# Another order for the start of a fused attention and two-MoE kernel: the first pair of heads, zero matmuls, planner keys

## The chip, the cores and the metric

The kernel runs on one core of a Trainium2 chip. The metric is the device time of one execution in microseconds (us), lower is better. Engines are named as in the profile: PE (TensorE, with PEld for its weight loads), DVE (VectorE), ACT (ScalarE), POOL (GpSimd) and SP (SyncE, which here issues nearly all DMAs).

## The reference, cut to what matters

```python
q_rot, k_rot = rotate(q), rotate(k)            # (4, 8, 576, 64): 4 batches, 8 heads
scores = (q_rot @ k_rot.T) / sqrt(64)
attn = softmax(scores)                          # over the keys
x = (attn @ v), heads put side by side          # (2304, 512)
x = relu(x @ w_in) ** 2 @ w_out                 # dense layer, 512 -> 2048 -> 512
e = argmax(x @ w_gate)                          # 8 experts, one for each token
y = gate * eom * (relu(x @ w1[e]) @ w2[e])      # 512 -> 1024 -> 512
```

`rotate` multiplies by cosines and sines of the position. All is float32; the kernel splits most operands into a high and a low part in a shorter format ("fp32r" in the rows) and multiplies high by high, high by low and low by high.

## The kernel before, in words

**Attention.** The 32 heads are taken as 16 pairs. `prepare(p)` (L272) makes a pair's operands, `unit(P, p, c)` (L405) works on one chunk of its queries (five chunks a pair, `QC`). For a pair, `prepare` loads k and q transposed, 128 partitions by 576 (`load`, L281: k is slot 2 of the tile `x`, q slot 0), makes a copy with neighbouring partitions exchanged (`swap`, DVE, L289), multiplies both with the table of cosines and the table of sines (`mul`, twice each, L292) and adds (`add`, L296). For all pairs but the first the multiplications and the addition run on POOL, for the first on DVE. Then k is split: `high_k` on ACT and `low_k` on POOL write the tile `hl`, and `fan` (L328), four DMAs of 288 KB a pair, copies both parts to the two halves of the partitions of the operand tile `d`. q is split straight into `d` (`high_q`, `low_q`). v is loaded, split in the same way (`v_high`, `v_low`), and two small copies `ends_` fill the tile `dz` for the last chunk. The first pair differs: its k goes without `fan`; four ACT casts (`first_high`, L320, 64 partitions each) and four DVE subtractions (`first_low`, L324) write all quarters of `d` directly. Both tables come in one DMA of 576 KB (L287), and one ACT instruction scales them for q (L335).

**A unit.** Four matmuls of 288 columns make the scores of one head (`scores`, L416, two PSUM buffers), DVE takes the least (`least`, L435), ACT the exponential (L439), PE transposes the result by the tile `ident` (L473, L479), ACT and DVE evacuate it as high and low part (L487, helper lines L209 and L212), and PE multiplies with v (L572).

**After the attention.** The dense layer runs over five blocks of tokens (`add_block`, L731). The first block's input is loaded and put together by POOL (L770 to L783) once all pairs are prepared, since it takes the place of the preparing tiles (`gate0`, L1415). Its weights come as raw words and are converted by ACT and DVE in the attention's shadow (`add_conversion`, L665). Then come routing and the experts.

**The order of the work** is made by a planner (`Plan`, L125). Every piece of work is added with its engine, an assumed cost, a key, what it depends on, and the buffers (rings) it uses. `emit` plays the pieces through: whichever engine is free first takes, among its pieces that are ready by then plus a small allowance, the one with the least key:

```python
t = max(free.get(e, 0.0), min(ready[n] for n in some))
n = min((ops[n][3], n) for n in open_[e] if ready[n] <= t + AHEAD.get(e, 0))[1]
```

The result is only an order of instructions for each engine. On the chip each engine runs its own list strictly in that order, and waits at an instruction whose data isn't there. The keys are `KEYS[class]` plus a small number that rises with the pair and the chunk, so a class with a lower value in `KEYS` goes ahead of another whenever both are ready. `fanned` (L344, L388, L657) is a dependency for the planner alone: loads of later pairs and of the constants follow the first pair's rotated k in the plan. The constants' split (`split`, L648, on DVE) is one piece with an assumed cost of 0.8 us.

Of the kernel before, what the change touches and what calls it, by code (L numbers as in the profile page):

```python
# [9 lines left out]
F32 = mybir.dt.float32  # L10
# [5 lines left out]
AF = mybir.ActivationFunctionType  # L16
# [5 lines left out]
B, H, S, D = 4, 8, 576, 64  # L22
# [33 lines left out]

def f32(ap):
    return ap.bitcast(F32)
# [6 lines left out]
def dve(n):  # L65
    return 67 + n / 0.96


def dves(n):
    return Shared(dve(n))  # L70
# [6 lines left out]
def act(n):  # L77
    return 93 + n / 1.2
# [6 lines left out]
def pool2(n):  # L85
    return 130 + 2.18 * n
# [18 lines left out]
def sub_price(on, n):  # L105
    return ("DVE", dves(n)) if on == "v" else ("POOL", pool2(n))
# [18 lines left out]
class Plan:  # L125
# [72 lines left out]
def two_moe_kernel(ctx, tc, qk, v, tab, cst, w_in, w_out, wg, w1, w2, out):  # L198
    nc = tc.nc
    te, ve, se, po, sp = nc.tensor, nc.vector, nc.scalar, nc.gpsimd, nc.sync  # L200
# [10 lines left out]
    def sub(eng, out, a, b):  # L211
        eng.tensor_tensor(out=out, in0=a, in1=b, op=ALU.subtract)  # L212
# [7 lines left out]
    pools, rings, plan = {}, {}, Plan()  # L220
# [8 lines left out]
    ident = rt.tile([128, 128], F32, name="ident")  # L229
# [20 lines left out]
    def add_attention(ctx, rest, first):  # L250
# [4 lines left out]
        ps_1 = pool(ctx, "ps_1", 1, space=PSUM)  # L255
# [3 lines left out]
        tabs = pre.tile([128, 4, S], F32, name="tabs")  # L259
# [9 lines left out]
        ring_z = plan.ring(1)  # L269
        zeros = [plan.add("DVE", 150, lambda: ve.memset(f32(ends_q), 0.0), -1000, [], [])]  # L270

        def prepare(p):  # L272


# [45 lines left out]
            def first_high(j, u):  # L320
                h, o = slice(64 * j, 64 * j + 64), slice(64 * u, 64 * u + 64)
                se.copy(out=operand()[o, j, 1], in_=T["x"][h, 2])

            def first_low(j, u):  # L324
                h, o = slice(64 * j, 64 * j + 64), slice(64 * u, 64 * u + 64)
                sub(ve, operand()[o, j, 2], T["x"][h, 2], f32(T["d"][h, j, 1]))
# [10 lines left out]
            on, split = ("vvvvvv", "aavvap") if first else (choice(ROPE, p, 6), choice(SPLIT, p, 6))  # L337
            eng = lambda i: ve if on[i] == "v" else po
            price = lambda i: ("DVE", dves(S)) if on[i] == "v" else ("POOL", pool2(S))
            hls, ds = ring_hl.take(), ring_d.take()  # L340
            parts = {}
            for i in (1, 0):
                k = key + KEYS["rope"] - i
                o = plan.add("SP", 3670 if first and i else 1220, lambda i=i: load(i), key + KEYS["load"] - i, fanned, [xs])  # L344
                if first and i:
                    tables = plan.add("ACT", act(2 * S), scale_tables, key + KEYS["qk"], [o], [])
                ready = [tables] if first and not i else []
                m = [plan.add("DVE", dve(S), lambda i=i: swap(i), key + KEYS["swap"] - i, [o], [xs])]
                m.append(plan.add(*price(3 * i), lambda z=2 * i: mul(z), k, [o, m[0], *ready], [xs]))
                m[0] = plan.add(*price(3 * i + 1), lambda z=2 * i + 1: mul(z), k, [m[0], *ready], [xs])  # L350
                o = plan.add(*price(3 * i + 2), lambda i=i: add(i), k, m, [xs])
                k = key + KEYS["qk"] - i
                if i and first:
                    T["fan"] = []
                    for j in range(2):
                        made_ = []
                        for u in range(2):
                            a = plan.add("ACT", act(S), lambda j=j, u=u: first_high(j, u), k, [o], [xs, ds])
                            made_ += [a, plan.add("DVE", dves(S), lambda j=j, u=u: first_low(j, u), k, [a], [xs, ds])]
                        T["fan"].append(made_)  # L360
                    fanned.append(o)
                elif i:
                    a = plan.add(*copy_price(split[1], S), high_k, k, [o], [xs, hls])
                    b = plan.add(*sub_price(split[3], S), low_k, k, [a], [xs, hls])
                    T["fan"] = [[plan.add("SP", 2444, lambda j=j: fan(j), key + KEYS["fan"], [a, b], [hls, ds])] for j in range(2)]
                else:
                    T["q"] = []
                    for j in range(2):
                        e = split[0] + split[2] if j == 0 else SECOND[2 * (p % (len(SECOND) // 2)):][:2]
                        if first:  # L370
                            e = "av" if j else "av"
                        a = plan.add(*copy_price(e[0], S), lambda j=j, e=e: high_q(j, e[0]), k, [o], [xs, ds])
                        b = plan.add(*sub_price(e[1], S), lambda j=j, e=e: low_q(j, e[1]), k, [a], [xs, ds])
# [14 lines left out]
            r = plan.add("SP", 1430, load_v, key + KEYS["load"], fanned, [vrs])  # L388
# [220 lines left out]
        made = {0: prepare(0), 1: prepare(1)}  # L609
        for p in range(NP):  # L610
            P = made.pop(p)
            for c in range(5):
# [956 lines left out]
```

## Time and profile before

| | us |
|---|---|
| median of 3 runs (975.94 to 977.5) | 976.64 |
| the profiled execution's own time | 977.0 |
| its span, first to last instruction | 975.2 |
| PE busy / DVE / ACT / POOL in it | 926.7 / 684.9 / 549.2 / 364.0 |

In the profile a row of a timeline has the start, the time taken by a run of equal instructions, engine, line, operation, output and inputs, their number, and in brackets how long the engine had been idle before it and what ended that. Rows by window have the busy time of each engine in a stretch, the clock granted to PE, the busy share of the 16 DMA engines, and GB/s. Two or more instructions in one row overlap at their ends. Lines L209, L212 and L207 are helpers that many steps share, so there the tile's name tells the step.

### The profile page before, as it was taken

Reading aid. Unit: us, or ns where it says so; the run is one execution under the profiler, and the core shown is the slowest. Engines: PE = TensorE matmul, PEld = TensorE weight load, DVE = VectorE, ACT = ScalarE, POOL = GpSimd, SP = SyncE. Lnnn points to the kernel's source line nnn. Section 1 sums busy time; section 2 is a strip of 40 time slices with the busy share of each in tenths; the row PEclk is TensorE's granted clock in tenths of the full one; section 3 lists DMA queues with packets and bytes.
Section 4 is the critical chain, followed back from the end, with each engine's and each line's share of the span. In section 5 each row is a group of like instructions: output and inputs, shape, how many; then the busy total and the mean of one; then the engine's idle time right before and its main releaser. Section 6 shows DMA issues by size and latency. Waiting matters only on the chain.

```text
span 975.2 us, 16438 instructions
## 1 busy us (share of the span) xinstructions
PE 926.7 (95%) x5612; PEld 814.2 (83%) x5612; DVE 684.9 (70%) x1272; ACT 549.2 (56%) x1154; POOL 364.0 (37%) x297
## 2 busy tenths in 40 slices
PE   1899999999999999999999999999999999999995
PEld 1799999998988887778777877888998889999995
DVE  7888999999997996542354244354678998266666
ACT  3899999999996895222232233223443555244443
POOL 4799999999862000000000000000131553134353
PEclk9999999999999999999999999999999999999998
DMA  4378777857584760410130012000640613352521
GB/s 140 92 189 218 190 206 184 210 149 189 145 238 143 252 202 20 133 39 1 41 109 14 0 30 69 1 5 29 240 161 33 238 45 117 121 182 81 197 69 36
DMA packets 55865, 115.94 MB, mean 119 GB/s; under 512 B 9025, under 2 KB 18769, under 8 KB 55761
## 3 DMA queue, kind: packets, MB, share of 16 engines
q1 hardware_dynamic: 52480, 104.17, 36.2%
q0 software_dynamic: 3280, 10.49, 3.2%
q8 instruction: 52, 0.85, 0.4%
q14 instruction: 53, 0.43, 0.1%
HBM read 98.96 MB, written 19.21 MB: 121 GB/s over the span
## 4 chain that ended last, share of the span: by engine, by line
PE 71%; DVE 11%; ACT 7%; DMA 3%; POOL 3%; issue 3%; SPq 0%; DVEq 0%; POOLq 0%; ACTq 0%
PE h L806 20%; PE a L836 19%; PE h L1324 10%; PE a L1361 9%; PE sc L422 3%; PE ov L578 3%; ACT pt L443 3%; PE tp L477 3%; DVE pg L212 2%; ACT phi L209 2%; DVE plo L212 1%; DVE mx L437 1%; DMA x<-qk_dram 1%; DMA xhi<-rd 1%; POOL d L212 1%
## 5 line engine op out<-in xcount | busy, mean ns | idle before, releaser
L806 PE MATMUL h<-xhi,pg 128*128 128x512 f32 (+1 forms) x640 | 198.8, 374 | 0.0
L836 PE MATMUL a<-gh,pg 128*128 128x512 f32 (+1 forms) x640 | 196.3, 373 | 0.0
L1278 POOL DMA_INDIRECT raw<-x1d,gidx x22 | 22.9, 1041 | 374.7 <-DVE ssc L243 358.1
L813 ACT ACTIVATE r<-h 128x512 f32<-128x512 f32 (+1 forms) x80 | 44.4, 554 | 197.1 <-PE h L806 184.8
L806 PEld LDWEIGHTS h<-xhi,pg 128*128 128x128 f32 x640 | 117.3, 188 | 23.1
L836 PEld LDWEIGHTS a<-gh,pg 128*128 128x128 f32 x640 | 117.2, 188 | 22.1
L821 DVE TENSOR_TENSOR r<-r 128x512 f32<-128x512 f32 (+1 forms) x64 | 40.5, 633 | 125.6 <-ACT gh L817 125.6
L422 PE MATMUL sc<-d 128*128 128x288 f32 x512 | 99.4, 317 | 26.7 <-DVE d L212 18.9
L836 PE MATMUL a<-gl,pg 128*128 128x512 f32 (+1 forms) x320 | 119.7, 374 | 2.7 <-DVE gl L212 2.4
L806 PE MATMUL h<-xlo,pg 128*128 128x512 f32 (+1 forms) x320 | 118.9, 372 | 0.0
L1324 PE MATMUL h<-raw,pg 128*128 128x256 f32 x960 | 117.9, 283 | 0.9 <-DVE ht L1333 0.8
L1324 PEld LDWEIGHTS h<-raw,pg 128*128 128x128 f32 x960 | 116.8, 190 | 2.2 <-PE m L876 1.0
L437 DVE TENSOR_REDUCE mx<-sc 128x1 f32<-128x576 f32 x144 | 107.0, 748 | 9.2 <-PE sc L422 5.9
L443 ACT ACTIVATE pt<-sc,mx 128x576 f32<-128x576 f32 x144 | 107.6, 748 | 7.4 <-DVE mx L437 6.4
L422 PEld LDWEIGHTS sc<-d 128*128 128x128 f32 x512 | 74.8, 193 | 32.8 <-DVE d L212 19.3
L212 DVE TENSOR_TENSOR plo<-tp,phi 128x512 fp32r<-128x512 f32 x144 | 94.9, 678 | 4.5 <-ACT phi L209 4.4
L212 DVE TENSOR_TENSOR pg<-pg,pg 128x512 fp32r<-128x512 f32 x102 | 95.1, 960 | 3.1 <-ACT pg L209 2.9
L294 POOL TENSOR_TENSOR x<-x,tabs 128x576 f32<-128x576 f32 x60 | 86.5, 1462 | 7.6 <-DVE x L290 6.5
L477 PE MATMUL tp<-ident,pt 128*128 128x128 f32 x576 | 86.4, 277 | 2.3 <-DVE plo L212 2.0
L209 ACT CAST phi<-tp 128x512 fp32r<-128x512 f32 x144 | 82.2, 585 | 4.2 <-PE tp L477 2.8
L212 POOL TENSOR_TENSOR pg<-pg,pg 128x512 fp32r<-128x512 f32 x34 | 45.7, 1353 | 86.2 <-ACT pg L209 82.5
L836 PEld LDWEIGHTS a<-gl,pg 128*128 128x128 f32 x320 | 60.3, 188 | 16.4 <-DVE gl L212 5.7
(216 smaller groups left out, 1736.9 us busy)
## 6 DMA issues: line engine op xcount, KB each, us to landing
pg<-w_dram SPq DMA_DIRECT2D x176, 256.0 KB
d<-hl SPq DMA_DIRECT2D x60, 288.0 KB
x<-qk_dram SPq DMA_DIRECT2D x32, 288.0 KB
xtd<-xt SPq DMA_DIRECT2D x32, 288.0 KB
raw<-w_in_dram SPq DMA_DIRECT2D x16, 512.0 KB
raw<-w_out_dram SPq DMA_DIRECT2D x16, 512.0 KB
vr<-v_dram SPq DMA_DIRECT2D x16, 352.0 KB
x1d<-b SPq DMA_DIRECT2D x18, 256.0 KB
```

Of the source, the lines that this page charges most:

```text
L209: (ve.tensor_copy if on == "v" else se.copy)(out=out, in_=in_)
L212: eng.tensor_tensor(out=out, in0=a, in1=b, op=ALU.subtract)
L294: eng(3 * (i // 2) + i % 2).tensor_tensor(out=x[:, i], in0=x[:, i], in1=tabs[:, i], op=ALU.mult)
L422: te.matmul(out=t[:, hf, 0:HB], lhsT=ends_q[:, 1] if both else d[:, j, 0, q0 + 64 * j:q0 + 64 * j + n], rhs=d[:, 1 if both else j, part, z ...
L437: ve.tensor_reduce(out=T["mx", j], in_=T["s", j][:, :, 0:HB], axis=AX.XY, op=ALU.min)
L443: se.activation(out=T["pt"][:, j].rearrange("p (a b) -> p a b", a=2), in_=T["s", j][:, :, 0:HB], func=AF.Exp, bias=T["mx", j], scale=-1.0, ...
L477: te.transpose(out=t[:, k], in_=T["pt"][:, j, i:i + 128], identity=ident)
L806: te.matmul(out=G["t"], lhsT=a[:, 128 * c:128 * c + 128], rhs=m[:, c, :n], start=c == 0 and i == 0, stop=c == KC - 1 and i == 2,)
L813: se.activation(out=G["r"], in_=G["t"], func=AF.Relu)
L836: te.matmul(out=T["acc", d][:, :n], lhsT=a[:, 128 * d:128 * d + 128], rhs=m, start=f == 0 and i == 0, stop=f == NF - 1 and i == 2,)
L1324: te.matmul(out=T["t"][:, f], lhsT=m[:, z], rhs=r[:, c], start=i == 0, stop=i == 11)
L1361: te.matmul(out=T["t"], lhsT=a[:, k, 128 * i:128 * i + 128], rhs=m, start=k == 0 and y == 0, stop=k == KF - 1 and y == 2,)
```

## The change

The first pair gets an order of its own (`HEAD` instead of `KEYS` for its load, swap, rope, qk and fan). Its k is now split as in the other pairs: one ACT cast and one DVE subtraction of 128 partitions, then `fan`. The tables come in two DMAs of 288 KB and are scaled in two ACT instructions; the sines no longer hold up the product with the cosines. In the plan the second pair's swaps depend on the first pair's first split of q (`after_first`), the first pair's `v_high` on its second, and the first two pairs' x loads no longer depend on `fanned`, which is now the first pair's rotated q. `ident` is loaded ahead of all else. PE begins with `warm`: 22 matmuls of 128x128 by 256 columns of zeros, 16 transposes of 64x64 and 4 of 128x128, 46 more matmuls of 256 columns, all into the PSUM tiles `ov` and `rem`, whose first use comes later. `KEYS`, `AHEAD`, `TAIL` and `LATE` get new values, `AHEAD` one for SP as well.

```diff
-TAIL, LATE = -3990153, -5019554
+TAIL, LATE = -4036178, -5122628
-AHEAD = dict(ACT=198, DVE=58, POOL=97)
+AHEAD = dict(ACT=86, DVE=59, POOL=107, SP=52)
+FIRST = "aavvap"
+HEAD = dict(load=-4000000, swap=-4000000, rope=-3000000, qk=-3500000, fan=-3000000)
-KEYS = dict(fan=-8426144, swap=-541378, step=14820833, conv=2741046, x0=-3160398, end=-2138599, load=-9529041, rope=18931248, qk=-3455, v=2543709, s=-1077225, min=-5182488, exp=-60406, rc=-3586704, t=5073609, hi=-2768973, lo=-3224226, pv=6609959, x=-3517649)
+KEYS = dict(fan=-10044688, swap=6989776, step=-784364, conv=11192405, x0=-10176758, end=9807859, load=-1091568, rope=12010027, qk=3046451, v=-8228284, s=-15791617, min=-2634065, exp=2258146, rc=-11490668, t=5989439, hi=1733607, lo=-1147514, pv=8583316, x=-463011)
...
+        loaded = plan.add("SP", 270, lambda: sp.dma_start(out=ident, in_=cst[:, 0:128]), -5000000, [], [])
+
+        def warm():
+            z = ends_q.rearrange("p j q -> p (j q)")
+            a, b = (ps_1.tile([128, 512], F32, tag=t, name=n) for t, n in (("o", "ov"), ("rem", "rem")))
+
+            def one(t, rows):
+                te.matmul(out=t[:, 0:256], lhsT=ends_q[rows, 0], rhs=z[rows], start=True, stop=True)
...
+            for i in range(22):
+                one((a, b)[i % 2], every)
+            for i in range(8):
+                turn(a, low, i)
+                turn(b, high, i)
+            for i in range(4):
+                te.transpose(out=a[:, 128 * i:128 * i + 128], in_=y[:, 0], identity=ident)
+            for i in range(46):
+                one((a, b)[i % 2], every)
+
+        plan.add("PE", 11500, warm, -5000000, zeros + [loaded], [ring_o.take(), ring_rem.take()])
...
-                if first and i:
-                    sp.dma_start(out=tabs[:, 2:4], in_=tab)
+
+            def load_table(z):
+                sp.dma_start(out=tabs[:, 2 + z], in_=tab[:, z])
...
-            def scale_tables():
-
-                se.activation(out=tabs[:, 0:2], in_=tabs[:, 2:4], func=AF.Copy, scale=-(D ** -0.5))
+            def scale_table(z):
+
+                se.activation(out=tabs[:, z], in_=tabs[:, 2 + z], func=AF.Copy, scale=-(D ** -0.5))
+
+            def order(name, more=0):
+                return (HEAD[name] if first else key + KEYS[name]) + more
...
+            after_first = made[0]["q"][0] if p == 1 else []
...
-                o = plan.add("SP", 3670 if first and i else 1220, lambda i=i: load(i), key + KEYS["load"] - i, fanned, [xs])
+                o = plan.add("SP", 1220, lambda i=i: load(i), order("load", -i), [] if p < 2 else fanned, [xs])
...
-                m = [plan.add("DVE", dve(S), lambda i=i: swap(i), key + KEYS["swap"] - i, [o], [xs])]
+                m = [plan.add("DVE", dve(S), lambda i=i: swap(i), order("swap", -i), [o] + after_first, [xs])]
...
-                if i and first:
-                    T["fan"] = []
-                    for j in range(2):
-                        made_ = []
-                        for u in range(2):
-                            a = plan.add("ACT", act(S), lambda j=j, u=u: first_high(j, u), k, [o], [xs, ds])
-                            made_ += [a, plan.add("DVE", dves(S), lambda j=j, u=u: first_low(j, u), k, [a], [xs, ds])]
-                        T["fan"].append(made_)
-                    fanned.append(o)
-                elif i:
+                if i:
                     a = plan.add(*copy_price(split[1], S), high_k, k, [o], [xs, hls])
                     b = plan.add(*sub_price(split[3], S), low_k, k, [a], [xs, hls])
-                    T["fan"] = [[plan.add("SP", 2444, lambda j=j: fan(j), key + KEYS["fan"], [a, b], [hls, ds])] for j in range(2)]
+                    T["fan"] = [[plan.add("SP", 2444, lambda j=j: fan(j), order("fan", j), [a, b], [hls, ds])] for j in range(2)]
...
+            if first:
+                T["rotated"] = o
+                fanned.append(o)
...
-            a = plan.add(*copy_price(split[4], 11 * D), v_high, key + KEYS["v"], [r] + zeros, [vrs, vs])
+            a = plan.add(*copy_price(split[4], 11 * D), v_high, key + KEYS["v"], [r] + zeros + (T["q"][1] if first else []), [vrs, vs])
...
-        plan.add("SP", 780, lambda: sp.dma_start(out=ident, in_=cst[:, 0:128]), 0, [], [])
```

## Rows read from the trace of the kernel before

**Rows 1.** Windows: busy PE, PEld, DVE, ACT, POOL; granted clock, DMA share, GB/s.

```profile
30.82:100.00 69.18, 66.92 (x517) 63.58 (x516) 60.72 (x107) 65.73 (x161) 67.42 (x56) 1.00 0.68 178
100.00:200.00 100.00, 98.52 (x761) 94.22 (x760) 97.41 (x165) 98.46 (x241) 94.86 (x78) 1.00 0.75 196
200.00:274.84 74.84, 69.90 (x536) 65.77 (x535) 72.09 (x114) 70.59 (x169) 68.44 (x56) 1.00 0.64 167
...
300.00:350.00 50.00, 50.00 (x222) 40.93 (x221) 43.09 (x77) 40.66 (x72) 0.00 (x0) 1.00 0.68 211
```

**Rows 2.** Timeline of POOL at the end of the preparing, and of PE after it.

```profile
274.39 0.45 POOL L207 TENSOR_SCALAR dz<-d 128x64 fp32r<-128x64 f32 x2 [0.54 <-PE sc L430]
...
296.53 1.29 POOL L212 TENSOR_TENSOR xlo<-xr,xhi 128x512 fp32r<-128x512 f32 x1 [0.36 <-DVE xhi L780]
...
298.32 0.39 PE L806 MATMUL h<-xhi,pg 128*128 128x512 f32 x1
```

**Rows 3.** Timeline of SP: the first load, and a fan of a later pair.

```profile
0.72 0.41 SPq L285 DMA_DIRECT2D x<-qk_dram  x1
...
32.27 3.53 SPq L331 DMA_DIRECT2D d<-hl  x4
```

**Rows 4.** Timeline of DVE from the start to the second and third minimum.

```profile
0.86 0.27 DVE L270 MEMSET dz<- 128x256 f32 x1 [0.86 <-PEq L1559]
...
3.88 0.79 DVE L290 STREAM_SHUFFLE x<-x 128x576 f32<-128x576 f32 x1
5.37 1.43 DVE L294 TENSOR_TENSOR x<-x,tabs 128x576 f32<-128x576 f32 x2 [0.70 <-DMA tabs<-tab_dram]
...
8.32 1.52 DVE L212 TENSOR_TENSOR d<-x,d 64x576 fp32r<-64x576 f32 x2 [0.74 <-ACT d L322]
...
16.97 3.24 DVE L212 TENSOR_TENSOR d<-x,d 64x576 fp32r<-64x576 f32 x2
...
20.91 1.48 DVE L650 CAST trib<-m 128x256 bf16<-128x256 f32 x1
...
25.44 1.35 DVE L437 TENSOR_REDUCE mx<-sc 128x1 f32<-128x576 f32 x2
```

**Rows 5.** Timeline of ACT: the first pair's k, and the second pair's k.

```profile
7.62 2.73 ACT L322 CAST d<-x 64x576 fp32r<-64x576 f32 x4 [1.17 <-DVE x L298]
...
30.08 0.67 ACT L209 CAST hl<-x 128x576 fp32r<-128x576 f32 x1
```

**Rows 6.** Windows: a stretch in which a fan's four DMAs move.

```profile
36.00:38.00 2.00, 2.00 (x19) 2.00 (x18) 1.60 (x3) 1.98 (x5) 1.92 (x2) 1.00 1.00 240
```

**Rows 7.** Timeline of PE: scores; last row, from the chain: 256 columns late.

```profile
18.38 1.33 PE L422 MATMUL sc<-d 128*128 128x288 f32 x4 [18.38 <-DVE d L212]
...
27.05 0.93 PE L422 MATMUL sc<-d 128*128 128x288 f32 x4 [3.07 <-ACT pt L443]
...
28.69 1.31 PE L422 MATMUL sc<-d 128*128 128x288 f32 x4
...
284.61 0.79 PE L422 MATMUL sc<-d 128*128 128x288 f32 x4 [0.72 <-ACT pt L443]
...
753.90 5.74 PE h L1324 x48
```

**Rows 8.** Windows: PE's clock at the start and when it rises.

```profile
28.00:30.00 2.00, 2.00 (x10) 1.99 (x9) 1.35 (x2) 1.34 (x5) 0.00 (x0) 0.50 0.00 0
31.00:32.00 1.00, 1.00 (x9) 0.77 (x7) 1.00 (x3) 0.84 (x3) 1.00 (x1) 1.00 0.00 0
```

**Rows 9.** Timeline of POOL: first work, the second pair, the wait for ACT.

```profile
11.23 2.21 POOL L212 TENSOR_TENSOR vh<-vr,vh 128x704 fp32r<-128x704 f32 x1 [10.80 <-ACT vh L209]
16.31 3.29 POOL L294 TENSOR_TENSOR x<-x,tabs 128x576 f32<-128x576 f32 x2 [2.87 <-DVE x L290]
...
23.88 2.75 POOL L294 TENSOR_TENSOR x<-x,tabs 128x576 f32<-128x576 f32 x2
30.82 1.42 POOL L212 TENSOR_TENSOR hl<-x,hl 128x576 fp32r<-128x576 f32 x1 [4.19 <-ACT hl L209]
```

More of the change, by code (lines that the diff above doesn't have):

```diff
@@ L270, in add_attention, with turn @@
         zeros = [plan.add("DVE", 150, lambda: ve.memset(f32(ends_q), 0.0), -1000, [], [])]
+        loaded = plan.add("SP", 270, lambda: sp.dma_start(out=ident, in_=cst[:, 0:128]), -5000000, [], [])
[4 more added lines that the diff above has]
+                te.matmul(out=t[:, 0:256], lhsT=ends_q[rows, 0], rhs=z[rows], start=True, stop=True)
+            every, low, high = slice(0, 128), slice(0, 64), slice(64, 128)
+            y = f32(ends_q)
+            def turn(t, rows, i):
+                te.transpose(out=t[:, 64 * i:64 * i + 64], in_=y[rows, 0], identity=ident[rows, rows])
+            for i in range(22):
[8 more added lines that the diff above has]
+        plan.add("PE", 11500, warm, -5000000, zeros + [loaded], [ring_o.take(), ring_rem.take()])
         def prepare(p):
@@ L318, in low_q @@
                 sub(ve if on == "v" else po, T["d"][o, j, 0], T["x"][h, 0], f32(T["d"][h, j, 0]))
[L320 to L326, printed above, removed]
             def fan(j):
@@ L331, in fan @@
                     sp.dma_start(out=f32(operand()[u:u + 64, j, 1:3]), in_=f32(T["hl"][h]))
-            def scale_tables():
-                se.activation(out=tabs[:, 0:2], in_=tabs[:, 2:4], func=AF.Copy, scale=-(D ** -0.5))
-            on, split = ("vvvvvv", "aavvap") if first else (choice(ROPE, p, 6), choice(SPLIT, p, 6))
+            def scale_table(z):
+                se.activation(out=tabs[:, z], in_=tabs[:, 2 + z], func=AF.Copy, scale=-(D ** -0.5))
+            def order(name, more=0):
+                return (HEAD[name] if first else key + KEYS[name]) + more
+            on, split = ("vvvvvv", FIRST) if first else (choice(ROPE, p, 6), choice(SPLIT, p, 6))
             eng = lambda i: ve if on[i] == "v" else po
             price = lambda i: ("DVE", dves(S)) if on[i] == "v" else ("POOL", pool2(S))
+            after_first = made[0]["q"][0] if p == 1 else []
             hls, ds = ring_hl.take(), ring_d.take()
@@ L342, in prepare @@
             for i in (1, 0):
-                k = key + KEYS["rope"] - i
-                o = plan.add("SP", 3670 if first and i else 1220, lambda i=i: load(i), key + KEYS["load"] - i, fanned, [xs])
+                o = plan.add("SP", 1220, lambda i=i: load(i), order("load", -i), [] if p < 2 else fanned, [xs])
                 if first and i:
-                    tables = plan.add("ACT", act(2 * S), scale_tables, key + KEYS["qk"], [o], [])
-                ready = [tables] if first and not i else []
@@ L348, in prepare @@
-                m = [plan.add("DVE", dve(S), lambda i=i: swap(i), key + KEYS["swap"] - i, [o], [xs])]
[L349 to L352, printed above, removed]
-                if i and first:
-                    T["fan"] = []
-                    for j in range(2):
-                        made_ = []
-                        for u in range(2):
-                            a = plan.add("ACT", act(S), lambda j=j, u=u: first_high(j, u), k, [o], [xs, ds])
-                            made_ += [a, plan.add("DVE", dves(S), lambda j=j, u=u: first_low(j, u), k, [a], [xs, ds])]
-                        T["fan"].append(made_)
-                    fanned.append(o)
-                elif i:
+                    t = [plan.add("SP", 1220, lambda z=z: load_table(z), HEAD["load"], [], []) for z in range(2)]
@@ new lines, in prepare @@
+                    tables = [plan.add("ACT", act(S), lambda z=z: scale_table(z), HEAD["swap"], [t[z]], []) for z in range(2)]
+                ready = (t if i else tables) if first else [None, None]
+                m = [plan.add("DVE", dve(S), lambda i=i: swap(i), order("swap", -i), [o] + after_first, [xs])]
+                m.append(plan.add(*price(3 * i), lambda z=2 * i: mul(z), order("rope", -i), [o, m[0], ready[0]], [xs]))
+                m[0] = plan.add(*price(3 * i + 1), lambda z=2 * i + 1: mul(z), order("rope", 1 - i), [m[0], ready[1]], [xs])
@@ L363, in prepare @@
+                o = plan.add(*price(3 * i + 2), lambda i=i: add(i), order("rope", 1 - i), m, [xs])
+                k = order("qk", -i)
+                if i:
                     a = plan.add(*copy_price(split[1], S), high_k, k, [o], [xs, hls])
                     b = plan.add(*sub_price(split[3], S), low_k, k, [a], [xs, hls])
-                    T["fan"] = [[plan.add("SP", 2444, lambda j=j: fan(j), key + KEYS["fan"], [a, b], [hls, ds])] for j in range(2)]
+                    T["fan"] = [[plan.add("SP", 2444, lambda j=j: fan(j), order("fan", j), [a, b], [hls, ds])] for j in range(2)]
@@ L370, in prepare @@
                         if first:
-                            e = "av" if j else "av"
-                        a = plan.add(*copy_price(e[0], S), lambda j=j, e=e: high_q(j, e[0]), k, [o], [xs, ds])
-                        b = plan.add(*sub_price(e[1], S), lambda j=j, e=e: low_q(j, e[1]), k, [a], [xs, ds])
+                            e = "av"
+                        a = plan.add(*copy_price(e[0], S), lambda j=j, e=e: high_q(j, e[0]), k + j, [o], [xs, ds])
+                        b = plan.add(*sub_price(e[1], S), lambda j=j, e=e: low_q(j, e[1]), k + j, [a], [xs, ds])
                         T["q"].append([a, b])
+            if first:
+                T["rotated"] = o
+                fanned.append(o)
             vs, vrs = ring_vh.take(), ring_vr.take()
@@ L386, in v_low @@
                 sub(ve if split[5] == "v" else po, T["v"][:, :, D:], T["vr"], f32(T["v"][:, :, 0:D]))
-            r = plan.add("SP", 1430, load_v, key + KEYS["load"], fanned, [vrs])
-            a = plan.add(*copy_price(split[4], 11 * D), v_high, key + KEYS["v"], [r] + zeros, [vrs, vs])
+            r = plan.add("SP", 1430, load_v, key + KEYS["load"], [] if first else fanned, [vrs])
+            a = plan.add(*copy_price(split[4], 11 * D), v_high, key + KEYS["v"], [r] + zeros + (T["q"][1] if first else []), [vrs, vs])
             T["vl"] = plan.add(*sub_price(split[5], 11 * D), v_low, key + KEYS["v"], [a], [vrs, vs])
@@ L605, in values @@
                 stored.append((o, P["stored"]))
-        plan.add("SP", 780, lambda: sp.dma_start(out=ident, in_=cst[:, 0:128]), 0, [], [])
         prepared, stored, begin, fanned, scored = [], [], [], [], []
-        made = {0: prepare(0), 1: prepare(1)}
+        made = {}
+        for p in range(2):
+            made[p] = prepare(p)
         for p in range(NP):
```

## The prediction

> **What bounds the kernel now.** The windows come first, since shares over the whole span average over two halves. From 300 us on PE alone is full and POOL does nothing, while from 31 to 275 us PE, DVE, ACT and POOL all have nine tenths or nearly so [rows 1]. The attention is four engines side by side, and whichever is last sets its end. Part of what ACT and DVE do there is weight conversion, which has the lowest rank and fills gaps; POOL has no such filler, so its idle time is waiting: 1.8 us from 31 to 100, 5.1 to 200, 6.4 to 275 [rows 1].
>
> The end of the stage is read from the timelines of POOL and PE: the last preparing ends at 274.84, the first block's input is complete when POOL ends at 297.82, and PE begins the dense layer at 298.32 [rows 2]. So what POOL gains before 275 us comes through to PE, and from there on PE is full and the rest moves with it.
>
> The timelines of the start have the holes. PE makes no score before 18.38 [rows 7]. POOL starts on the second pair at 16.31, and then stands still for 4.19 us before 30.82, waiting for an ACT cast at 30.08 [rows 5, 9]. ACT runs it behind exponentials, and these wait for DVE, which splits constants from 20.91 to 25.44, a piece that the planner prices at 0.8 us [rows 4].
>
> **The change, part by part.** *Loads.* `ident` ahead of the first load costs one issue, some 0.4 us [rows 3]; the k swap moves from 3.88 to about 4.3. The cosines are half of what had to land, so the 0.70 us wait of the first product goes, or at worst stays [rows 4]. Swap, two products and a sum at a product's price (0.79, 1.43, 0.72) then end at about 7.4 with the handovers, against 7.5: nothing either way [rows 4].
>
> *k of the first pair.* Four ACT casts (2.73 us) and four DVE subtractions (1.52 for two, twice) become one and one; an instruction on 128 partitions takes what one on 64 takes, 0.67 on ACT and so 0.76 on DVE [rows 4, 5]. DVE saves 2.3 us, ACT 2.0. What is added is `fan`. Four such DMAs are issued from 32.27, and the DMA engines are full until 38 [rows 3, 6], so some 5.5 us for both heads and 3 for the first. On SP they stand behind loads that wait for nothing; behind them are v of the second pair and the constants, which nobody needs yet.
>
> *Order.* In `HEAD` q's swap ranks before k's split, and that before q's products. From 7.4 DVE has the swap (0.79), k's subtraction (0.76), two products and a sum (2.2), ending at 11.2; ACT casts q (0.67), DVE subtracts (0.76 each): the first head's q is there at 12.7, the second's at 13.5. The last two subtractions took 3.24 us before, with POOL at work beside them, against 1.52 without [rows 4, 9]; holding back the second pair keeps POOL quiet here. The fan leaves at 9.0: first head 12, second 14.5.
>
> *Zeros.* PE can begin when DVE has cleared `dz`, at 1.2 [rows 4]. Four score matmuls take 1.31 us at 28.69, where the granted clock is 0.50 (1.2 GHz), and 0.79 late, at 2.4; those at 18.38 took 1.33, so they ran at the lower level [rows 7, 8]. PE worked without a break from 27.05 and had the full clock at 31 [rows 7, 8]. I take the same 4 us here, 16 matmuls at 0.25; 52 more at 5.74/48 = 0.12 are 6.2, and 20 transposes, no wider, 2.4 [rows 7]. The zeros end at 13.8, 1.1 behind the first head's q. The far ends are 88 instructions at 0.12 (11.8, hidden) and all of them at the lower level, below.
>
> So the first scores come at 13.8 instead of 18.38: PE, DVE's minima and ACT's exponentials lead by 4.6 us.
>
> *A rule to weigh.* At the full clock each group of four scores at the start saves 0.54 us; there are six until 31 us, so 3.2 us of PE at most, and nothing if the clock falls again [rows 7]. It fell before: PE was idle for 3.07 us ahead of 27.05 and at 0.50 by 28 [rows 7, 8]. The constants still hold up DVE for 4.5 us and will leave PE such a gap, so I count nothing beyond the first scores. The Trainium skill (TensorE: Matmul & The Clock Gate, Part 1) says that the low clock is the resting state, which activity releases and idleness brings back. By that rule the zeros' effect ends at the gap and the sum stays at 972.2; without it, it would be 969.0. The trace agrees with the rule, by the 0.50 at 28 us.
>
> *POOL.* Its second pair starts behind that pair's swap at 13.5 + 0.8 and a handover, 14.4 instead of 16.31: 1.9 us. But v's subtraction of the first pair, which lay in idle time (2.21 at 11.23), now waits for q and lies in POOL's line, at 1.7 to 2.2; I take 1.7, as it no longer meets DVE's subtractions [rows 9]. That leaves 0.2. The 4.19 us stall is bounded from both sides: it stays whole, or it goes. ACT ended it, and ACT leads by 4.6, so its end comes at 26.2; POOL's own work (to 26.63, less 0.2) ends at 26.4 [rows 9]. I take it as gone: POOL leads by 0.2 + 4.2 = 4.4 us. Late next is the second pair's q on ACT, again behind exponentials.
>
> *Keys.* On each engine the classes rank nearly as before: POOL v (was third), qk, end, rope; ACT rc, x, hi, exp, qk, conversions; PE scores and rc, then t, pv; DVE rc, minima, lo, swap, conversions; on SP the fan now goes ahead of x loads. `TAIL` and `LATE` keep their order. Really new are a negative `step` (of two weights being converted the later goes first, though rings hold them in line), the constants ranking before swaps, and ACT's smaller allowance. None adds work; all reshuffle POOL's 13.3 us of waits between 31 and 275 [rows 1]. I take zero, with an estimate of 3 us either way, a quarter of those waits.
>
> **Sum.** 4.4 us off the profiled execution's 977.0 gives 972.6; that execution lies 0.36 above the median, so 972.2. Less than 0.2% (2 us) can't be told from no change.
>
> **Rivals.** *POOL keeps its stall.* If the second pair's cast is queued behind more exponentials than before, or the constants' split falls just ahead of it, POOL waits as it did and only 0.2 us is left: 976.4. For it: the split isn't priced any better, and ACT's ranking is the same. Against: ACT is 4.6 us ahead. 12%.
>
> *Everything gains.* If the stall goes, the 1.7 us that the q subtractions lost beside POOL don't come back elsewhere, and half of the 3.2 us of PE is had, 3.3 to 3.7 us more comes off: 968.7. For it: DVE has 2.3 and ACT 2.0 us less to do. Against: the gap behind the constants. 12%.
>
> *The zeros outlast the loads.* PE works in order, so the scores stand behind all 88 instructions. If zeros leave the clock at its lower level, each takes between 0.24 (twice 0.12) and 0.30 us (1.33/4 cut to 256 columns), together 21 to 26, and the first scores come at 22 to 27, 4 to 9 us later than before [rows 7]. Every lane starts so much later; in the middle, 6 us less the 2.3 that DVE saves, 3.7 slower: 980.3. It decides once the zeros last beyond 18 us. For it: no row shows the clock under such matmuls. Against: it rose at 31 us under ordinary ones. 8%.
>
> **How the numbers follow.** The forecast has 68%; with *everything gains* that is 80% for faster by over 0.2%. *POOL keeps its stall* gives 12% for no change, the zeros 8% for slower. The forecast with 3 us of reshuffling and half a microsecond for the other terms reaches from 968.7 to 975.7; opened by half a microsecond below for the best case and to 976.5 above for the kept stall, it is 968.2 to 976.5 and leaves out the zeros and the outer parts of the others.
>
> **What would show it.** Right: zeros until about 14 us, first scores at 13.5 to 14.5, DVE's subtractions of q at 0.76 each, POOL's second pair at 14.4, its first `hl` at 26 to 27, preparing done near 270.5 and the dense layer begun near 294, all after it as before. Wrong: zeros still running when the second head's fan has landed, a POOL wait for ACT's `hl` or `d` of 3 us or more, the dense layer's start within 1 us of 298.3, or gaps on PE in the first block, where the reversed conversions would come late.

## The result, and the profile after

The changed kernel takes 990.23 us (median of 4 runs, 987.15 to 991.37) against 977.07 for the kernel before beside it: a ratio of 1.0129, with an interval of 1.0101 to 1.0157. It is slower, by 13.2 us, where 4.4 us less were forecast. The profiled execution took 989.41 us with a span of 987.3, 12.1 us over that of before.

The start went nearly as forecast, but for the fan. Timeline of PE (start, us, engine, line, operation, count, idle before and what ended it), the last of the first 22 zeros, two of the last 46, and the first scores:

```profile
5.62 0.41 PE L281 MATMUL ov<-dz 128*128 128x256 f32 x1
5.83 0.37 PE L281 MATMUL rem<-dz 128*128 128x256 f32 x1
...
12.55 0.28 PE L281 MATMUL ov<-dz 128*128 128x256 f32 x1
12.67 0.28 PE L281 MATMUL rem<-dz 128*128 128x256 f32 x1
14.52 0.77 PE L442 MATMUL sc<-d 128*128 128x288 f32 x4 [1.57 <-DMA d<-hl]
17.18 2.26 PE L442 MATMUL sc<-d 128*128 128x288 f32 x8 [1.90 <-DMA d<-hl]
...
20.20 1.33 PE L442 MATMUL sc<-d 128*128 128x288 f32 x4
```

The zeros come 0.21 us apart at first and 0.12 at last, so they did raise the clock, and end at 12.95. The first head's scores take the 0.77 us of the full clock at 14.52, against 1.33 at 18.38 before [rows 7]. But PE waits 1.57 and 1.90 us for the fan's two halves, which come at 14.52 and 17.18 instead of the forecast 12 and 14.5, and the second head's scores are slow again. PE's windows (busy PE, PEld, DVE, ACT, POOL, granted clock, DMA share, GB/s) show both, the clock and the full DMA engines:

```profile
14.00:17.00 3.00, 0.77 (x4) 0.56 (x4) 2.08 (x4) 0.98 (x3) 2.21 (x2) 0.88 0.99 250
17.00:20.00 3.00, 2.82 (x12) 2.72 (x12) 1.28 (x2) 0.69 (x2) 3.00 (x3) 0.50 0.91 264
20.00:25.00 5.00, 4.75 (x25) 4.13 (x24) 4.50 (x10) 4.05 (x12) 4.69 (x5) 0.69 0.10 38
```

Then the lead is lost on its way to POOL. Timeline of DVE, the constants' split:

```profile
24.71 1.23 DVE L671 CAST trib<-m 128x256 bf16<-128x256 f32 x1
25.86 1.68 DVE L672 CAST wgh<-m 128x64 fp32r<-128x64 f32 x1
27.58 1.35 DVE L214 TENSOR_TENSOR wgh<-m,wgh 128x64 fp32r<-128x64 f32 x1
```

Timeline of ACT, the exponential held up behind it, and the second pair's q:

```profile
29.74 0.74 ACT L463 ACTIVATE pt<-sc,mx 128x576 f32<-128x576 f32 x1 [3.43 <-DVE mx L457]
...
35.13 1.36 ACT L211 CAST d<-x 64x576 fp32r<-64x576 f32 x2
```

Timeline of POOL, the second pair and, far below, the end of the first block's input:

```profile
14.79 1.40 POOL L324 TENSOR_TENSOR x<-x,tabs 128x576 f32<-128x576 f32 x1 [14.35 <-DVE x L320]
...
24.38 1.41 POOL L214 TENSOR_TENSOR hl<-x,hl 128x576 fp32r<-128x576 f32 x1 [0.31 <-ACT hl L211]
...
35.93 2.91 POOL L214 TENSOR_TENSOR d<-x,d 64x576 fp32r<-64x576 f32 x2 [5.73 <-ACT d L211]
...
301.67 1.28 POOL L214 TENSOR_TENSOR xlo<-xr,xhi 128x512 fp32r<-128x512 f32 x1 [0.36 <-DVE xhi L801]
```

POOL begins the second pair at 14.79 and its wait for `hl` shrinks from 4.19 [rows 9] to 0.31 us. The lead that I forecast (4.4 us) is there: 6.4 us at that instruction, of which 1.7 come from v's subtraction for the second pair, which now stands behind `hl` instead of ahead of it. Four instructions later POOL waits 5.73 us for the second pair's q. ACT runs its list in order, q stands there behind exponentials, and these waited 3.43 us for minima that stood on DVE behind the constants' split. The wait removed came back, longer, one step on. Over the first 40 us (windows, columns as above) POOL is then busy for 19.20 us, against 21.36 before, and DVE for 28.35 against 32.10:

```profile
0.00:40.00 40.00, 31.32 (x201) 29.00 (x202) 28.35 (x49) 20.84 (x45) 19.20 (x18) 0.87 0.57 154
...
100.00:200.00 100.00, 93.94 (x709) 87.63 (x708) 97.27 (x159) 93.63 (x229) 93.59 (x76) 1.00 0.73 195
```

The n-th exponential of the scores on ACT serves as a milestone. How much later (+) or earlier it ends than in the kernel before, in us, for the changed kernel and for runs told of below:

| n | 1 | 10 | 37 | 55 | 73 | 100 | 118 | 144 | dense layer begins |
|---|---|---|---|---|---|---|---|---|---|
| kernel before, ends at | 21.7 | 42.6 | 92.1 | 125.4 | 157.3 | 208.3 | 243.3 | 292.8 | 298.32 |
| changed kernel | -4.8 | -1.6 | -1.8 | -0.5 | +3.3 | +5.9 | +4.3 | +4.0 | +4.8 |
| new keys alone (e1_keys) | +4.4 | +1.4 | -0.8 | +3.5 | +6.9 | +11.7 | +12.8 | +15.8 | +24.9 |
| first pair's order alone (e6_firstonly) | -4.6 | -4.7 | -3.3 | -2.9 | +1.6 | +0.7 | +1.2 | +2.5 | +3.8 |
| changed, no zeros (e3_nowarm) | -3.8 | -2.4 | -2.5 | -1.0 | +2.9 | +5.4 | +3.8 | +3.3 | +4.1 |
| the same, split moved (e13_moved) | -4.1 | -6.3 | -6.4 | -5.1 | -2.4 | +0.2 | -1.4 | -0.8 | 0.0 |
| before, split moved (e14_movedb) | +1.1 | -2.4 | -2.7 | -2.7 | -2.7 | -2.8 | -2.8 | -2.5 | -2.4 |

So 4.8 of the span's 12.1 us are lost by the start of the dense layer. Of the other 7.3, most lies in the last unit. Timeline of PE, the dense layer's first matmul and the last unit:

```profile
303.09 0.39 PE L827 MATMUL h<-xhi,pg 128*128 128x512 f32 x1
...
944.73 9.96 PE L1382 MATMUL a<-pg,ht 128*128 128x512 f32 x42
957.20 13.15 PE L1345 MATMUL h<-raw,pg 128*128 128x256 f32 x96 [2.52 <-issue]
```

The same rows of the changed kernel without its zeros have neither the gap nor the slow matmuls:

```profile
944.82 9.26 PE L1381 MATMUL a<-pg,ht 128*128 128x512 f32 x39
953.92 11.68 PE L1344 MATMUL h<-raw,pg 128*128 128x256 f32 x96
```

In the changed kernel PE stands still for 2.52 us and waits for no engine and no data ("issue"), its granted clock falls (0.70 from 957.2 to 960, 0.78 from 960 to 964), and the 96 matmuls behind take 1.47 us more: 4.0 us together.

### The profile page after: what moved, and what is told of

It reads as the page before. It is cut to its first block, busy times and chain, and to the rows that moved or that the text cites. A ratio compares the mean times of both kernels' runs of the same rounds, so it can differ in the third digit from the quotient of the medians.

```text
span 987.3 us, 16637 instructions
## 1 busy us (share of the span) xinstructions
PE 944.2 (96%) x5700; PEld 828.2 (84%) x5700; DVE 685.2 (69%) x1269; ACT 543.8 (55%) x1152; POOL 363.0 (37%) x297
## 4 chain that ended last, share of the span: by engine, by line
PE 68%; DVE 14%; DMA 6%; ACT 5%; issue 3%; POOL 2%; SPq 1%; DVEq 0%; POOLq 0%; ACTq 0%
PE h L827 19%; PE a L857 18%; PE h L1345 9%; PE a L1382 8%; PE sc L442 4%; PE tp L497 3%; DVE pg L214 3%; PE ov L598 3%; DMA xr<-xtd 2%; ACT pt L463 2%; ACT phi L211 2%; DVE plo L214 2%; DVE mx L457 2%; DMA d<-hl 2%; DVE pg L211 1%
## 5 line engine op out<-in xcount | busy, mean ns | idle before, releaser
L457 DVE TENSOR_REDUCE mx<-sc 128x1 f32<-128x576 f32 x144 | 106.1, 745 | 11.7 <-PE sc L442 8.7
L214 DVE TENSOR_TENSOR pg<-pg,pg 128x512 fp32r<-128x512 f32 x102 | 92.4, 933 | 3.1 <-ACT pg L211 2.9
L497 PEld LDWEIGHTS tp<-ident,pt 128*128 128x128 f32 x576 | 68.3, 142 | 13.9 <-issue 6.6
```

The source lines that it names most:

```text
L457: ve.tensor_reduce(out=T["mx", j], in_=T["s", j][:, :, 0:HB], axis=AX.XY, op=ALU.min)
L497: te.transpose(out=t[:, k], in_=T["pt"][:, j, i:i + 128], identity=ident)
```

## The experiments

The expectations name theories by letters: K the new keys, F the first pair's order, C the place of PE's code; later ones explain their own. Ratios are to the kernel before, with the 95% interval; it had medians of 977.1 to 978.2 us.

**New keys alone.** The kernel before with the four new lines.

```diff
-TAIL, LATE = -3990153, -5019554
+TAIL, LATE = -4036178, -5122628
-AHEAD = dict(ACT=198, DVE=58, POOL=97)
+AHEAD = dict(ACT=86, DVE=59, POOL=107, SP=52)
...
```

> The kernel before with the new KEYS, AHEAD, TAIL and LATE alone; first pair and start as before. Theory K (the new keys order the attention worse, the first pair's order gains about 4 us and loses it again): 982 to 990, with the first exponential near 21.7 us and the dense layer beginning at 305 to 310. Theory F (the first pair's order puts the constants' split and POOL's waits in a bad place, the keys are neutral): 975 to 979. Theory C (88 more matmuls move the later code, and its fetching stalls PE at the end): 977, no stall near 950.

1002.71 us, ratio 1.0243 (1.0221 to 1.0264). The dense layer begins at 323.23 us:

```profile
323.23 0.77 PE L806 MATMUL h<-xhi,pg 128*128 128x512 f32 x1
```

The instructions are the same and equal in number; the order alone costs 24.9 us by then, far more than theory K had (982 to 990 us, dense layer at 305 to 310). On this start the new keys are much worse than the old ones.

**Old keys on the new start.** The changed kernel with the three old lines and `HEAD` put below them.

```diff
-HEAD = dict(load=-4000000, ...
+HEAD = dict(load=-12000000, ...
```

> The changed kernel with the old KEYS, AHEAD, TAIL and LATE (HEAD's load set under the old load key, so that the first loads keep their place). Theory K: 970 to 975, dense layer beginning near 294. Theory F: 986 to 991, POOL's wait of 5 us or more after its second pair still there. Theory C: 980 to 982, PE's gap near 950 still there.

981.59 us, 1.0035 (1.0021 to 1.0049); dense layer at 302.19. That is 8.6 us better than the change, though the dense layer begins only 0.9 us sooner; the rest comes later, where the gap in the last unit, for one, is 1.43 us instead of 2.52. The time and the gap are as theory C had them. And the keys are not all of it: with the old ones the new start is slower than the kernel before, too.

**No zeros.**

```diff
-        plan.add("PE", 11500, warm, -5000000, zeros + [loaded], [ring_o.take(), ring_rem.take()])
```

> The changed kernel without the zero matmuls. Theory K and theory F: within 1.5 us of the changed kernel (988 to 991), first scores at 14.5 at half the pace, dense layer beginning within 1 us of 303. Theory C: 984 to 987, the gap of 2.5 us on PE near 955 gone.

985.31 us, 1.0072 (1.0053 to 1.0091). Without zeros the first exponential comes 1.0 us later, the tenth 0.7 us sooner and the dense layer 0.7 us sooner (302.42); and the gap in the last unit is gone, as shown above. That is theory C again. In the changed kernel the zeros cost 4.9 us, most of it 950 us after they ran.

**Zeros alone, and with another number.** The kernel before with `ident` first and the 88 zeros of the change, and then with 128 of them:

```diff
-            for i in range(46):
+            for i in range(86):
                 one((a, b)[i % 2], every)
```

> The kernel before with the zero matmuls and the identity loaded first, nothing else. Theories K and F: within 1 us of the kernel before (976 to 978): the zeros end at 12.6, the scores still come at 18.4 to 19. Theory C: 980 to 982 with a gap of 2 us or more on PE in the experts' last units.

> As the zeros on the kernel before (984.39), with 40 more zero matmuls: 128 matmuls with their weight loads are 256 instructions, and PE's instruction fetches in the trace are 16 KB each, one every 256 instructions of 64 bytes. Theory C (the zeros cost by where they leave later code within such blocks): back to 976 to 979, no gap on PE after the last branch, although there are more zeros. Rival Z (the zeros cost by themselves, by clock, power or queue): 984 to 988.

984.39 us, 1.0067 (1.0044 to 1.009), and 979.26 us, 1.0011 (0.9999 to 1.0023). Theory C's gap came with 88 zeros and not with 128, and both times are a little above its bounds (by 2.4 and 0.3 us); the second is far from rival Z's 984 to 988. Timeline of PE in the last unit, with 88 zeros:

```profile
948.40 0.52 PE L1350 MATMUL h<-raw,pg 128*128 128x256 f32 x3
951.10 11.41 PE L1350 MATMUL h<-raw,pg 128*128 128x256 f32 x93 [2.17 <-issue]
```

and with 128:

```profile
937.59 11.44 PE L1387 MATMUL a<-pg,ht 128*128 128x512 f32 x48
948.88 11.68 PE L1350 MATMUL h<-raw,pg 128*128 128x256 f32 x96
```

Forty more zeros are faster, by 5.1 us of the medians. Each zero is a matmul and a weight load; 88 are 176 instructions, 128 are 256. In the page's list of DMA queues the instruction fetches stand by themselves (packets, MB, share):

```profile
q8 instruction: 52, 0.85, 0.3%
```

0.85 MB in 52 packets is 16 KB each. If an instruction has 64 bytes, an estimate from 256 leaving PE's code as it was, a packet holds 256, and 256 more instructions leave all later code at the same place in its packets, where 176 move it. The fetches by themselves don't differ: in the changed kernel a packet is fetched at 954.81, behind the last branch (to 954.1), and in the kernel before at 947.09, as far behind that branch (to 946.4), but there PE has code to go on with. Of the runs here, all those with 88 zeros have a gap of this kind, and none with 0 or 128. The more matmuls PE still runs after the branch, the shorter the gap: 0, 3, 10, 14 and 18 of them go with 2.52, 2.17, 1.43, 0.99 and 0.78 us (changed kernel, e4_warm, e2_oldkeys, e7_vend, e8_ahead). That is what code running out at the end of a packet would give; where the packets end is not in the traces. Nor do the zeros cost the same everywhere: on the new start with the old keys the time is 981.59 us with them (e2_oldkeys) and 983.62 without (e6_firstonly), with intervals that overlap.

**The first pair's order alone,** that is, the old keys and no zeros.

> The first pair's order alone: old KEYS, AHEAD, TAIL and LATE, no zeros. If the zeros cost some 5 us by the code's place and the first pair's order gains little net: 975 to 978, first exponential 4 us earlier than before, dense layer beginning 2 to 4 us later or at the same time. If the first pair's order is what loses: 981 or more. If it gains what was predicted: 971 to 974.

983.62 us, 1.0053 (1.0035 to 1.007). The lead of 4.6 us holds to the tenth exponential, is 2.9 at the 55th, and is gone by the 73rd (table); the dense layer begins at 302.15. By the expectation this is the case in which the first pair's order itself loses. The constants' split is not what does it here: it falls into a wait of POOL (3.19 us, for `hl`) and takes 0.7 us.

**Two of the new keys put back,** `v` and `end`, whose ranks had changed most, **and the old allowances.**

In the changed kernel `end` becomes -2138599 and `v` 8000000 in the one run; in the other

```diff
-AHEAD = dict(ACT=86, DVE=59, POOL=107, SP=52)
+AHEAD = dict(ACT=198, DVE=58, POOL=97)
```

> The changed kernel with two keys put back to their old rank on POOL: v between qk and rope, end ahead of qk. If these two ranks are what makes the new keys slow: 981 to 985, dense layer beginning near 298 to 300. If it is the allowances or the conversions: 988 to 992.

> The changed kernel with the old AHEAD (ACT 198, DVE 58, POOL 97, none for SP). If the allowances are what makes the new plan slow: 981 to 985. If the keys: 987 to 992.

995.7 us, 1.0175 (1.0149 to 1.0202), dense layer at 315.01; and 986.22 us, 1.0092 (1.0071 to 1.0113), at 304.94. With the two old keys it is worse than either case had it, and the old allowances come out between their two cases: the time falls by 4.0 us, but the dense layer begins 1.85 us later, so what they gain lies behind it. Neither is what makes the dense layer late. With the old allowances a lead of 2.5 us at the 100th exponential is lost again by the 144th (+3.8).

**Orders found with better prices, and the split done twice.** The first two are the new start without zeros, the third is the kernel before, each with new values in the lines of keys alone. The fourth is the changed kernel without zeros and with three more lines in `split`:

```diff
+            ve.tensor_copy(out=trib, in_=C["t"].rearrange("p (a b) -> p a b", a=2))
+            ve.tensor_copy(out=wgh[:, :, 0], in_=w)
+            sub(ve, wgh[:, :, 1], w, f32(wgh[:, :, 0]))
```

> The new start without the zeros, with KEYS, AHEAD, HEAD, TAIL and LATE found by a local search from the new values. What is searched for is the end of the planner's order when it is replayed with five sets of prices: the planner's own, and with what the trace showed added step by step (constants' split 4.3 us instead of 0.8, a pair's swap 0.79 us instead of 0.667, a POOL operation 0.03 and 0.06 us longer). Mean of the five: 845.1 us, against 846.3 for the new keys and 847.3 for the kernel before with its own. Theory P (the time is lost by prices that are too low, and an order made with better ones takes it back): between 976 and 981 us, the dense layer beginning at 295 to 299 us. Theory S (the loss arises in the first 40 us, from late transfers and the constants' split, and no planning of the rest takes it back): 982 to 986 us, dense layer at 300 to 303 us.

> As the run before, but the search began at the old keys (mean of the five price sets 845.2 us, planner's own end 838.7 us, the lowest of all). Theory P: 976 to 981 us. Theory S: 982 to 986 us. If neither and it is above 988 us, the planner's end and its replay with better prices say little of the chip at this scale.

> The kernel before, with keys from the same search begun at its own (mean 846.5 us against 847.3 before). Theory P: 976 to 978 us, a gain of up to 1 us. If orders of equal planned length differ on the chip by several us whatever is changed, it is anywhere from 975 to 985 us.

> The changed kernel without the zeros, in which the constants' three copies on DVE are done twice (the second time over the first's result). The planner's order is the same to the last instruction. Theory P (a price that is too low passes through to the dense layer one for one, since the planned order has no slack): the copies take 3.5 to 4 us again, so the dense layer begins at 305.5 to 306.5 us instead of 302.4, and the time is 988.5 to 989.5 us against 985.3. Theory H (the copies lie beside waits and are hidden): dense layer at 302.4 to 303 us, time 985 to 986 us.

982.34 us, 1.0042 (1.0028 to 1.0056); 980.14, 1.0022 (1.0011 to 1.0033); 977.54, 0.999 (0.9977 to 1.0003). The time of the first lies in theory S, if at its edge, and its dense layer, at 303.75, is later than either theory had it; the times of the second and the third lie in theory P. New orders took back 3 to 5 us of the 7, and the one with the better result has its split later, at 30.14. The split done twice gave 986.25, 1.0081 (1.0063 to 1.01). By its median that is nearer to H, 0.9 us above the run without the doubling; by its profiled execution it is all but P (305.5 to 306.5), with the dense layer at 305.42 instead of 302.42 and 2.6 us more span. Timeline of DVE, the second copies:

```profile
28.44 1.50 DVE L673 CAST trib<-m 128x256 bf16<-128x256 f32 x1
29.87 0.18 DVE L674 CAST wgh<-m 128x64 fp32r<-128x64 f32 x1
30.08 0.22 DVE L214 TENSOR_TENSOR wgh<-m,wgh 128x64 fp32r<-128x64 f32 x1
```

Timeline of POOL in the same run, its wait for the second pair's q:

```profile
37.84 2.93 POOL L214 TENSOR_TENSOR d<-x,d 64x576 fp32r<-64x576 f32 x2 [8.04 <-ACT d L211]
```

and in the run without the doubling:

```profile
35.23 2.92 POOL L214 TENSOR_TENSOR d<-x,d 64x576 fp32r<-64x576 f32 x2 [4.54 <-ACT d L211]
```

The second copies take 1.9 us, and the first ones 4.5 instead of 3.3; DVE is done with them at 30.30 instead of 28.04. Those 2.3 us come out as 2.6 us by which POOL is later at q (its wait is 3.5 us longer), and 3.0 at the dense layer. And once POOL had stopped, at 29.8, the same copies took 0.18 and 0.22 us instead of 1.68 and 1.35: the split is long because of POOL beside it.

**The split moved.** The constants' loads and split are issued at an earlier place, and every other instruction stays where it is on its engine: on the changed kernel without zeros, on the kernel before, and on the second of the orders found. In the changed kernel the loads go behind the second pair's x (in `load`) and the split ahead of the first head's `low_q`; in the kernel before the loads go behind the first pair's v and the split ahead of `first_low(1, 0)`. The fourth run has the split as an early piece of the plan, and keys searched for that.

```diff
+                if p == 1 and i == 0:
+                    hooks["load"]()
...
+                if first and j == 0:
+                    hooks["split"]()
...
-        plan.add("DVE", 800, split, 0, [o], ms)
+        plan.add("DVE", 800, lambda: None, 0, [o], ms)
```

> The changed kernel without the zeros; the constants' loads are issued behind the second pair's x (at about 4.5 us instead of 16.3), and DVE splits them just ahead of its subtraction of the first head's q, where it waits for ACT and POOL has no work yet. Every other instruction keeps its place on its engine. Theory P (the split, held up beside POOL, is what takes the lead): the copies take 0.7 to 1 us in all, POOL's wait for the second pair's q falls from 4.5 us to 2 or less, the dense layer begins at 298.5 to 299.5 us instead of 302.4, and the time is 981 to 982.5 us instead of 985.3. Theory D (the loss is the later order and POOL's longer operations): the dense layer stays at 301.5 to 302.5 us, the time at 984.5 to 985.5 us.

> The kernel before with the same: the constants' loads go ahead of the second pair's x, and the split lies ahead of DVE's third subtraction of the first pair's k (at 10.4 us, where it waits 0.5 us for ACT and POOL is idle) instead of at 20.9 us. Nothing else moves. Theory P: DVE and with it ACT and POOL's first wait come 3 to 4 us sooner at 25 us, and 1.5 to 2.5 us of that reach the dense layer (a replay of the order with the chip's prices gives 1.7 to 2.2): 975.5 to 976.5 us against 978. Theory D: 977.5 to 978.5 us.

> e10_search3 with the same move as in e13_moved. There the split stood at 30.1 us. Theory P: 2.5 to 3.5 us less than e10_search3, so 976.5 to 977.7 us, with POOL's waits of 3.55 and 3.39 us before 30 and 39 us cut by that much together. Theory D: 979.5 to 980.5 us.

> The new start without zeros, constants loaded and split early as pieces of the plan with keys of their own in HEAD, and all keys found by the same search (mean of the five price sets 842.2 us, against 847.3 for the kernel before and 845.1 to 845.2 for the two orders found with the split in its old place). Theory P: 3 us below those two, so 976 to 979 us, and if the search's step over the kernel before (5 us) comes through, 973 to 976. Theory D: 980 to 983 us.

978.53 us, 1.0011 (0.9998 to 1.0023); **974.12, 0.9962 (0.995 to 0.9974)**; 977.14, 0.9992 (0.9976 to 1.0009); 975.94, 0.998 (0.9968 to 0.9992). Timeline of DVE in the first of them, the split:

```profile
11.67 0.28 DVE L674 CAST trib<-m 128x256 bf16<-128x256 f32 x1
11.87 0.18 DVE L675 CAST wgh<-m 128x64 fp32r<-128x64 f32 x1
12.09 0.23 DVE L214 TENSOR_TENSOR wgh<-m,wgh 128x64 fp32r<-128x64 f32 x1
```

and of POOL, its wait for the second pair's q:

```profile
31.30 2.92 POOL L214 TENSOR_TENSOR d<-x,d 64x576 fp32r<-64x576 f32 x2 [1.02 <-ACT d L211]
```

In the changed kernel the copies take 0.7 us, POOL's wait falls from 4.54 to 1.02, the dense layer begins at 298.28 instead of 302.42, and the time falls by 6.8 us, a part of it in the blocks and units behind. In the kernel before, the same move brings its first wait from 4.19 [rows 9] to 1.16 and the dense layer from 298.32 [rows 2] to 295.93. There the constants' loads were issued from 4.02 us on already and move by 1 us, so it is the split's place that counts. Timeline of POOL:

```profile
28.93 1.41 POOL L212 TENSOR_TENSOR hl<-x,hl 128x576 fp32r<-128x576 f32 x1 [1.16 <-ACT hl L209]
```

The first matmul of the dense layer:

```profile
295.93 0.39 PE L811 MATMUL h<-xhi,pg 128*128 128x512 f32 x1
```

This is the fastest version, 4 us below the kernel before, with neither the new start nor new keys; 2.4 of them are there at the dense layer. Theory P holds: the first two gained more than its bounds, the third lies within them (though of its two waits only the second went, the first is still 3.49 us), and the fourth is at the border between its two cases.

## Why the prediction was wrong

*What held.* Loads, k, order and zeros came nearly as worked out: zeros to 12.95 us (forecast 13.8), first scores at 14.52 (13.8), POOL's second pair at 14.79 (14.4), q's subtractions 1.53 us for two (0.76 each), the first `hl` at 24.38 (26 to 27). The fan was mis-sized: 5.0 us from its issue at 9.50 to the first scores and 7.7 to the second head's, against 3 and 5.5, with the DMA engines 0.99 busy from 14 to 17 us. That the first scores were only 0.7 us late is luck: the zeros, which were to set their time, ended 0.85 us early.

*The step that failed first is "I take it as gone: POOL leads by 0.2 + 4.2".* The wait for `hl` went, but "late next is the second pair's q on ACT, again behind exponentials" was named and priced at nothing. It was 5.73 us, longer than the wait removed. The rival *POOL keeps its stall* had the mechanism ("the constants' split falls just ahead of it"), but for the cast of k, not for that of q. The runs show it: e13_moved, where only the split and its loads move, brings the wait from 4.54 (without zeros) to 1.02 and the dense layer forward by 4.1 us. I had the 4.5 us of the split in the rows and the planner's 0.8 beside them [rows 4], and used them for PE's clock and for the rivals, not for the sum.

*The second is "what POOL gains before 275 us comes through to PE", and with it **Keys**, "I take zero, with an estimate of 3 us either way".* It holds for an order that stays as it is: what moving the split gains by the 37th exponential (2.7 us in e14_movedb, 3.9 between e3_nowarm and e13_moved) is there at the dense layer, to within 0.3. An order made anew gives a lead back. With the split out of the way and no zeros, the changed kernel is 6.4 us ahead at the 37th exponential, 5.1 at the 55th, and level at the dense layer (e13_moved); the first pair's order with the old keys goes from 3.3 us ahead to 3.8 late (e6_firstonly). On the new start the new keys are hardly worse than the old, since the dense layer begins at 302.42 and 302.15 (e3_nowarm, e6_firstonly); on the old start they cost 24.9 us.

Why the new orders lose there isn't settled: the windows from 100 to 200 us show PE at 93.94 and ACT at 93.63 busy against 98.52 and 98.46 [rows 1], so engines wait for each other more. One thing lines up with it, though no run tests it alone: where the weight conversions on DVE fall. One kind of them from 90 to 215 us (count, then least, median and longest in ns), before and after:

```profile
L698 DVE SCALAR_TENSOR_TENSOR b<-m,b x4: 676/820/1255, 101.9 to 188.6; 128x512 int32<-128x512 int32 x4
L719 DVE SCALAR_TENSOR_TENSOR b<-m,b x6: 682/1522/2043, 116.0 to 207.5; 128x512 int32<-128x512 int32 x6
```

Between the 55th and the 100th exponential the kernel before has 12 conversions on DVE, which take 13.0 us. The changed kernel has 16, which take 20.2 us, and loses 6.4 there; e13_moved has 16 in 18.0 and loses 5.3; e6_firstonly has 15 in 14.6 and loses 3.6. Next to no time is lost with 12 in 12.9 (e14_movedb), 8 in 9.8 (e8_ahead) or 3 in 4.5 (e15_moved3). e8_ahead loses 9.1 us behind the 100th, with 21 of them in 23.5 us there against 15 in 17.0 before. So these fillers may cost what the prediction put at nothing.

*The third is that zeros outside the start cost nothing,* "all after it as before". In the changed kernel they cost 4.9 us, most of it by the gap in the last unit. No rival had it; *the zeros outlast the loads* did not come.

*The rule.* The Trainium skill (TensorE: Matmul & The Clock Gate, Part 1) says that idleness brings the low clock back. The trace agrees: after PE's waits of 1.57 and 1.90 us the granted clock is 0.50 from 17 to 20 us. Counting nothing for the zeros beyond the first scores was right, and even those 1.0 us were lost again by the tenth exponential (e3_nowarm).

*The sum.* From the 37th exponential on: a lead of 6.4 us without the split, less 4.1 to 4.2 for the split beside POOL, less 0.7 for the zeros, less the 6.4 that e13_moved gives back by its order, is 4.8 to 4.9 late at the dense layer. Behind it come 4.0 in the last unit, and 3.3 in several places of the blocks and units, among them 1.86 us for which PE waits for DVE at 403 us. That makes 12.1.

## What to carry to other kernels

Before a wait is counted as gone, follow the waiting engine to its next instruction and price the wait there by the same cause; here one piece with a price five times too low fed both. Where an order is made by a planner, a new order is a change of its own: move one piece within the old order first, since that was carried to the dense layer nearly one to one, while new orders came out anywhere from -2 to +25 us. Instructions added to a program's start can cost time at its end, so compare the ends of the traces too.

## What the runs showed of the hardware that I had not expected

- After the last branch, where a 16 KB packet of instructions is fetched, PE stood still for 2.52 us in the changed kernel and 2.17 in the kernel before with 88 zeros; there 40 more matmuls, 950 us earlier, took the gap away. It looks as if PE ran out of code.
- Three small copies on DVE take 0.7 us with POOL idle and 3.3 to 4.5 us with POOL at work, although POOL works on other tiles; one of 64 columns took 1.68 us beside POOL and 0.18 without.
- Matmuls of zeros raise PE's clock: 0.21 us apart at the start, 0.12 from 7.4 us on, the 0.12 of others late in the run [rows 7]. In the first 14 us the granted clock reads 1.00 whatever the pace, so there the pace has to be read.
